# Raw weights requested as soon as their buffer is free, x loaded through ACT's queue, and fewer conversions inside the retention

## The chip, the cores and the metric

One Trainium2 chip, one of its cores. The metric is device time in microseconds (us) of one execution; smaller is better. The engines run their own instruction streams in order: TensorE (PE; its weight loads are PEld), VectorE (DVE), ScalarE (ACT), GpSimd (POOL) and SyncE (SP), which here issues the transfers.

## What is computed

Three parts follow one another on 2304 tokens (4 batches of 576) of width 512, all in float32:

```python
# 1. retention, per batch and head (8 heads of 64), gamma = 1 - 2 ** (-5 - head)
scores = q @ k.T / sqrt(64)
ret = (scores * where(i >= j, gamma ** (i - j), 0)) @ v      # -> x [2304, 512]
# 2. first feed-forward layer, w_in [512, 2048], w_out [2048, 512]
h = x @ w_in
x = (h * sigmoid(1.702 * h)) @ w_out
# 3. second feed-forward layer, w_in [512, 1024], w_out [1024, 512]
h = x @ w_in
s = h * softmax(h)
out = ((s - mean(s)) / sqrt(var(s) + 1e-6) * g_ln) @ w_out
```

The four weight matrices of parts 2 and 3 reach the core as float64, which it has to turn into float32 itself.

## The kernel before, in words

**Products.** Every operand of a matmul of parts 2 and 3 is split into a high part (a rounding copy on ACT, L291) and the rest (a subtraction on POOL or VectorE, L292), and a product is three matmuls: high x high, low x high, high x low. The up-projection is done with seven products in place of eight, on sums and differences of quarters of x and of w_in. Seven operands of x (`xop`, x0 to x6) belong to a pair of token tiles; seven combinations of w_in (`OPS`) to a slice of the weights, a window `win`.

**Steps.** Part 2 runs over 24 steps (`STEPS`): 4 generations of 4 slices of w_out, in each 3 pairs of token tiles, in each 2 halves i. A step emits h (`emit_h`: 7 products of 6 matmuls) and then y (`emit_y`: 48 matmuls; in the first two steps 24). The even step (i = 0) and the odd step (i = 1) of a pair read the same x0 to x6. During the odd step each xj becomes free after its own product; in generation 0 the next pair's xj is then computed there and stored to DRAM (`store_x`, L622), in generations 1 to 3 it is loaded back (`load_x`, L626): seven transfers of 768 KB, on SP. In h, VectorE makes the sums of products (L664) and the gated values (L638), ACT the sigmoid (L637), and ACT and POOL split the four gated tiles g11, g12, g21, g22.

**Weights.** float64 pieces of 128x512 (512 KB) are loaded by SP into one of two raw buffers (`load_raw`, L251) and turned into float32 by three integer instructions on VectorE (`convert`, L267, L270, L273), with a fourth for scaled ones. Combinations (L282), splits and, for part 3, spills of finished weights to DRAM (L392) follow.

**Order.** Each engine's order is the order in which the program emits. Background work stands in a list `bg` of (cost, function, needs, gives, late) and is emitted at calls of `slot(n)`: the head of the list goes out while its needs are done, and, if it has a cost, while n is above 0. An entry marked late is put aside and emitted first thing at the next call of `slot`. Before the change the load that refills a raw buffer is such a late entry, and so is every split and spill. `run` calls `slot` after h, after y, and in the retention's later rounds k.

**Retention.** Eight rounds k of two units (two heads each). From k = 4 on, `sums` prepares x's sums, `make_x` splits x0 to x6 for the first pair, and `slot` emits conversions.

Of the kernel before, what the change touches and what calls it, by code (L numbers as in the profile page):

```python
# [23 lines left out]
P = 128  # L24
# [80 lines left out]
RIGHT_PAD = 120  # L105
WIN = 7 * 256
# [40 lines left out]
class Build:  # L147
    def __init__(self, tc, ctx, att, consts, ident_in, w1, w2in, w2out, out):
# [13 lines left out]
        self.r2 = [rp.tile([P, LAST], F32, name="r2"), self.at(_M["c"] + _CC["qdec"][0], LAST)]  # L162
        self.dram = self.pool("dram", space=bass.MemoryType.DRAM)
# [194 lines left out]
    def next_raw(self, dst, scale=None, need=(), give=None):  # L358


        i = self.taken
        self.taken += 1
        self.queue_convert(self.raw(i), dst, scale, tuple(need) + (("raw", i),), give)
        if i + 2 < len(self.pieces):
            src = self.source(self.pieces[i + 2])
            self.add(0, lambda: self.load_raw(self.raw(i), src), (), ("raw", i + 2), True)
# [234 lines left out]
    def combine_x(self, p):  # L601
# [12 lines left out]
        def split(j, engine=None):  # L614
            x = self.xop[j]
            self.split(x[:, 0], x[:, 1], src[j], engine)
# [7 lines left out]
    def load_x(self, p, j):  # L624
        x = f32(self.xop[j].rearrange("r a k t -> r (a k t)"))
        self.nc.sync.dma_start(out=x, in_=self.xd[p][j])  # L626
# [15 lines left out]
    def emit_h(self, s):  # L642
# [44 lines left out]
        g11[2]()  # L687
        yield 3
# [16 lines left out]
        g21[0]()  # L705
        g21[1]()
# [255 lines left out]
    def run(self):  # L962
# [31 lines left out]
        def make_x(*js):  # L994
            for j in js:
                split_x(j, None)
                self.xready += 1
# [5 lines left out]
        for k in range(NPAIR):  # L1003
# [34 lines left out]
            else:  # L1038
# [7 lines left out]
                if k > 3:  # L1046
                    for _ in range((1, 1, 1, 1)[k - 4]):
                        sums.pop(0)()
                self.slot((0, 0, 0, 0, 3, 3, 3, 3)[k])
# [10 lines left out]
                if nxt:  # L1060
                    self.states(u + 3, pt)
                    self.last_masks(k + 1, ends[0])
                    self.slot(1 if k > 3 else 0)
# [9 lines left out]
            if k > 3:  # L1073
                make_x(*((), (0, 1), (2, 3), (4, 5, 6))[k - 4])

        self.open_right()
        self.slot(3)
        for g, p, i in STEPS:
# [7 lines left out]
            for j in self.emit_h(s):  # L1086
# [10 lines left out]
            self.done.add(("h", s))  # L1097
# [3 lines left out]
            if s == 0:  # L1101
                while self.first_loads:
                    load_w()
            slots = max(1, 2 * (5 - s % 6 - (g == GENS - 1)) + 2 - (g == GENS - 1))
            self.slot(7 if s == 0 else -(-self.left() // slots) + 1)
# [15 lines left out]
            self.slot(7 if s == 0 else self.left() // max(1, slots) if s + 2 < NSTEP else 0)  # L1121
# [133 lines left out]
```

## Time and profile before

| | before |
|---|---|
| median of 2 runs | 773.88 us (772.07 to 775.68) |
| profiled execution | 771.56 us, span 769.8 us |
| busy: PE, PEld, DVE, ACT, POOL | 675.1, 624.0, 533.0, 295.1, 324.1 us |
| granted clock of TensorE, mean | 0.938 of full speed |
| chain that ended last: PE, DMA, DVE | 47%, 14%, 9% of the span |
| loads of x (42 of 768 KB), median to landing | 8.7 us |
| raw w_in pieces (28 of 512 KB), median to landing | 5.0 us |

The profile is one execution; times count from its first instruction. A group of equal instructions shows their busy time, the mean of one, and the idle time of the engine before them with what ended it. The granted clock is the share of full speed (2.4 GHz) that TensorE had; 0.5 is the lower level. The chain is followed back from the last instruction, at each step to what released it. The DMA share is that of the core's 16 DMA engines.

### The profile page before, as it was taken

How to read it: one execution, taken by the hardware profiler on the slowest of the kernel's cores; microseconds unless marked ns; L12 is line 12 of the kernel's file. 1: busy time of each engine (PE TensorE's matmuls, PEld its weight loads, DVE VectorE, ACT ScalarE, POOL GpSimd, SP SyncE). 2: the span in 40 equal slices, each digit the busy share in tenths (PEclk: the TensorE clock that was granted, in tenths of full speed). 3: DMA queues.
4: the chain of work that ended last, by engine and by line, in shares of the span. 5: the costliest groups of instructions: out<-in, count | busy, mean ns of one | idle time of the engine just before them, and what ended most of it. 6: DMA issues, size and time to landing. Idle time of an engine off the chain costs nothing.

```text
span 769.8 us, 11333 instructions
## 1 busy us (share of the span) xinstructions
PE 675.1 (88%) x4326; PEld 624.0 (81%) x4326; DVE 533.0 (69%) x840; ACT 295.1 (38%) x606; POOL 324.1 (42%) x297
## 2 busy tenths in 40 slices
PE   8996567787997979997989998938989999999998
PEld 7986466787997979997989988838847888888887
DVE  3699884845556867775868656727738988778881
ACT  3564343452542333433322432314324543344431
POOL 3468662852544433453533524517513332133300
PEclk9998877898999989998999998969999999999999
DMA  9994454162136492162762283842493000000001
GB/s 346 410 376 169 175 229 164 68 259 86 39 120 249 142 357 90 55 256 112 265 242 83 61 335 110 330 148 110 157 418 125 15 17 26 28 29 29 27 28 42
DMA packets 30006, 121.78 MB, mean 158 GB/s; under 512 B 3328, under 2 KB 3840, under 8 KB 29952
## 3 DMA queue, kind: packets, MB, share of 16 engines
q1 hardware_dynamic: 29952, 121.06, 41.4%
q8 instruction: 34, 0.56, 0.3%
q14 instruction: 20, 0.16, 0.1%
HBM read 88.28 MB, written 32.77 MB: 157 GB/s over the span
## 4 chain that ended last, share of the span: by engine, by line
PE 47%; DMA 14%; DVE 9%; issue 4%; POOL 2%; ACT 2%; SPq 1%; ACTq 0%; POOLq 0%; DVEq 0%
PE o L884 13%; PE y L730 11%; PE h L794 9%; PE h_B L658 4%; PE h_C L658 4%; DMA mem<-in_w 4%; DMA mem<-in_w2out 3%; DVE mem L739 2%; PE h_D L658 2%; PE h_A L658 2%; PE zT L858 2%; DVE mem L270 2%; DVE mem L273 2%; DMA mem<-in_w2in 1%; DMA u<-wd 1%
## 5 line engine op out<-in xcount | busy, mean ns | idle before, releaser
L292 POOL TENSOR_TENSOR g<-mem,g 128x384 fp32r<-128x384 f32 x96 | 114.6, 1213 | 198.7 <-ACT g L291 188.1
L291 ACT CAST g<-mem 128x384 fp32r<-128x384 f32 x96 | 48.4, 514 | 87.9 <-DVE mem L638 87.0
L730 PE MATMUL y<-g,wo 128*128 128x384 f32 x432 | 78.2, 335 | 0.0
L730 PEld LDWEIGHTS y<-g,wo 128*128 128x128 f32 x432 | 75.6, 189 | 0.3 <-DVE mem L739 0.2
L292 POOL TENSOR_TENSOR win<-mem,win 128x256 fp32r<-128x256 f32 (+2 forms) x55 | 49.7, 933 | 56.0 <-ACT win L291 52.0
L267 DVE TENSOR_SCALAR mem<-mem 128x512 uint32<-128x512 uint32 x44 | 31.8, 723 | 55.2 <-DMA mem<-in_w 27.7
L638 DVE TENSOR_TENSOR mem<-mem 128x384 f32<-128x384 f32 x72 | 39.5, 576 | 30.1 <-ACT mem L637 30.1
L292 POOL TENSOR_TENSOR ws<-mem,ws 128x512 fp32r<-128x512 f32 (+1 forms) x36 | 44.2, 1240 | 35.2 <-ACT ws L291 35.2
L637 ACT ACTIVATE mem<-mem 128x384 f32<-128x384 f32 x72 | 36.1, 522 | 47.2 <-DVE mem L664 46.9
L658 PE MATMUL h_B<-x,win1dt.float32r 128*128 128x384 f32 x108 | 26.8, 388 | 24.3 <-DVE mem L664 16.3
L664 DVE TENSOR_TENSOR mem<-h_B,mem 128x384 f32<-128x384 f32 x48 | 26.6, 553 | 30.6 <-PE h_B L658 16.2
L794 PE MATMUL h<-ut,win 128*128 128x512 f32 x168 | 44.5, 396 | 3.0 <-DMA ut<-wdt 3.0
L270 DVE SCALAR_TENSOR_TENSOR mem<-mem 128x512 uint32<-128x512 uint32 x44 | 44.8, 1017 | 1.2
L800 DVE TENSOR_TENSOR mem<-h,mem 128x512 f32<-128x512 f32 x36 | 24.6, 688 | 30.1 <-PE h L794 17.5
L739 DVE TENSOR_TENSOR mem<-y,mem 128x384 f32<-128x384 f32 x72 | 35.7, 550 | 13.9 <-PE y L730 13.7
L658 PE MATMUL h_B<-x,win0dt.float32r 128*128 128x384 f32 x108 | 26.0, 383 | 20.8 <-DVE mem L664 20.6
L273 DVE SCALAR_TENSOR_TENSOR mem<-mem 128x512 uint32<-128x512 uint32 x44 | 43.1, 979 | 1.3
L658 PEld LDWEIGHTS h_B<-x,win1dt.float32r 128*128 128x128 f32 x108 | 21.7, 218 | 27.2 <-DVE mem L664 18.4
L884 PE MATMUL o<-u,zs 128*128 128x512 f32 (+1 forms) x171 | 41.7, 388 | 0.0
L282 DVE TENSOR_TENSOR mem<-mem 128x256 f32<-128x256 f32 (+2 forms) x49 | 40.7, 859 | 0.9
L730 PE MATMUL y<-g,wo0dt.float32r 128*128 128x384 f32 x216 | 40.7, 335 | 0.5 <-POOL g L292 0.5
L845 POOL TENSOR_TENSOR mem<-mem 128x1 f32<-128x1 f32 x18 | 10.3, 574 | 73.1 <-DVE mem L844 66.9
(144 smaller groups left out, 1629.2 us busy)
## 6 DMA issues: line engine op xcount, KB each, us to landing
x<-xd SPq DMA_DIRECT2D x42, 768.0 KB, 8.7
xd<-x SPq DMA_DIRECT2D x21, 768.0 KB, 3.9
mem<-in_w SPq DMA_DIRECT2D x28, 512.0 KB, 5.0
in<-in_att SPq DMA_DIRECT2D x16, 576.0 KB, 8.5
in<-in_att SPq DMA_DIRECT2D x16, 544.0 KB, 8.9
out<-mem SPq DMA_DIRECT2D x17, 256.0 KB, 2.0
mem<-in_w2out SPq DMA_DIRECT2D x8, 512.0 KB, 3.8
wd<-ws SPq DMA_DIRECT2D x8, 512.0 KB, 5.1
```

The lines of the kernel that those rows point to most:

```text
L270: lambda: nc.vector.scalar_tensor_tensor(high, high, 0xC0000000, x, ALU.bitwise_and, ALU.bitwise_or),
L273: lambda: nc.vector.scalar_tensor_tensor(x, low, 29, high, ALU.logical_shift_right, ALU.bitwise_or),
L282: self.nc.vector.tensor_tensor(o, a, b, ALU.subtract)
L291: self.nc.scalar.copy(hi, src)
L292: (engine or self.nc.gpsimd).tensor_tensor(lo, src, f32(hi), ALU.subtract)
L637: lambda: nc.scalar.activation(g, src, AF.Sigmoid, scale=1.702),
L638: lambda: nc.vector.tensor_tensor(g, src, g, ALU.mult),
L658: nc.tensor.matmul(o, w[:, c:c + P], x[j][:, m, k], start=(start and i == 0), stop=(stop and i == 5), skip_group_check=True,)
L730: nc.tensor.matmul(self.yps[m], w[:, c:c + P], gs[:, b], start=(begin and i == 0), stop=(end and i == 2),)
L739: nc.vector.tensor_tensor(y[:, m], self.yps[m], y[:, m], ALU.add)
L794: nc.tensor.matmul(o, a[:, l, k], w[:, m], start=(start and i == 0), stop=(stop and i == 5), skip_group_check=True,)
L884: nc.tensor.matmul(o[:, 0:n], z[:, a, k], w[:, b, p * n:(p + 1) * n], start=(k == 0 and i == 0), stop=(k == FB - 1 and i == 2),)
```

## The change

It does five things. (1) `next_raw`: the load that refills a raw buffer is emitted as soon as the conversion that read it has been emitted; only the mark that allows its conversion is put off to the next `slot`. (2) `load_x`: the 42 loads of x are issued by ACT in place of SP. (3) `emit_h` itself calls `slot`: once without budget after g11's split, which emits what was put off, and once with the budget of the step between g21's sigmoid and its product; the call after h is gone. (4) In the retention the background budgets go from 3, 3, 3, 3 (rounds 4 to 7) and 1, 1, 1 to 3, 3, 3, 0 and none, then 5 in place of 3 before part 2, and 8.4 and 6 in place of 7 and 7 in step 0; x0 to x6 are made in another order and earlier, and the last of the first raw loads go out ahead of step 0's stores. (5) x's subtraction is issued as two of 128x384 in place of one of 128x768, and 56 words of padding stand at the end of the retention's tiles.

```diff
+RET_PAD = 56
...
+        rp.tile([P, RET_PAD], F32, name="rpad")
...
         if i + 2 < len(self.pieces):
             src = self.source(self.pieces[i + 2])
-            self.add(0, lambda: self.load_raw(self.raw(i), src), (), ("raw", i + 2), True)
+            self.add(0, lambda: self.load_raw(self.raw(i), src))
+            self.add(0, lambda: None, (), ("raw", i + 2), True)
...
         def split(j, engine=None):
             x = self.xop[j]
-            self.split(x[:, 0], x[:, 1], src[j], engine)
+            a = src[j] if len(src[j].shape) == 3 else src[j].rearrange("r (k t) -> r k t", k=2)
+            self.nc.scalar.copy(x[:, 0], a)
+            for k in range(2):
+                (engine or self.nc.gpsimd).tensor_tensor(x[:, 1, k], a[:, k], f32(x[:, 0, k]), ALU.subtract)
...
         x = f32(self.xop[j].rearrange("r a k t -> r (a k t)"))
-        self.nc.sync.dma_start(out=x, in_=self.xd[p][j])
+        self.nc.scalar.dma_start(out=x, in_=self.xd[p][j])
...
-    def emit_h(self, s):
+    def emit_h(self, s, n_slot):
...
         g11[2]()
+        self.slot(0)
         yield 3
...
         g21[0]()
+        self.done.add(("h", s))
+        self.slot(n_slot)
         g21[1]()
...
                 if k > 3:
-                    for _ in range((1, 1, 1, 1)[k - 4]):
-                        sums.pop(0)()
-                self.slot((0, 0, 0, 0, 3, 3, 3, 3)[k])
+                    sums.pop(0)()
+                self.slot((0, 0, 0, 0, 3, 3, 3, 0)[k])
...
-                    self.slot(1 if k > 3 else 0)
+                    self.slot(0)
...
             if k > 3:
-                make_x(*((), (0, 1), (2, 3), (4, 5, 6))[k - 4])
+                make_x(*((1, 3), (0, 2), (4, 6), (5,))[k - 4])
 
         self.open_right()
-        self.slot(3)
+        self.slot(5)
...
-            for j in self.emit_h(s):
+            slots = max(1, 2 * (5 - s % 6 - (g == GENS - 1)) + 2 - (g == GENS - 1))
+            for j in self.emit_h(s, 8.4 if s == 0 else -(-self.left() // slots) + 1):
+                while s == 0 and self.first_loads:
+                    load_w()
...
-            self.done.add(("h", s))
             if g == 0 and i == 0 and after is not None:
                 for fn in sums[:3]:
                     fn()
-            if s == 0:
-                while self.first_loads:
-                    load_w()
-            slots = max(1, 2 * (5 - s % 6 - (g == GENS - 1)) + 2 - (g == GENS - 1))
-            self.slot(7 if s == 0 else -(-self.left() // slots) + 1)
...
-            self.slot(7 if s == 0 else self.left() // max(1, slots) if s + 2 < NSTEP else 0)
+            self.slot(6 if s == 0 else self.left() // max(1, slots) if s + 2 < NSTEP else 0)
```

TensorE's order is the same in both. Where the change moves instructions is shown at three places; lines are those of each kernel's own text.

First SP, from the end of generation 0's stores (`xd`) to the first spill (`wd`) in generation 1; `in_w` and `in_w2out` are raw weights, x<-xd the loads of x. Before:

```order
L622 DMA xd_6_152<-x_131 128x1536
L251 DMA mem<-in_w 128x1024 x5
L626 DMA x_125<-xd_0_139 128x1536
L626 DMA x_126<-xd_1_140 128x1536
L626 DMA x_127<-xd_2_141 128x1536
L626 DMA x_128<-xd_3_142 128x1536
L626 DMA x_129<-xd_4_143 128x1536
L626 DMA x_130<-xd_5_144 128x1536
L626 DMA x_131<-xd_6_145 128x1536
L251 DMA mem<-in_w 128x1024 x2
L251 DMA mem<-in_w2out 128x1024 x3
L392 DMA wd_0_111<-ws 128x1024
```

With the change:

```order
L628 DMA xd_5_152<-x_131 128x1536
L253 DMA mem<-in_w 128x1024
L628 DMA xd_6_153<-x_132 128x1536
L253 DMA mem<-in_w 128x1024 x6
L253 DMA mem<-in_w2out 128x1024 x3
L395 DMA wd_0_112<-ws 128x1024
L253 DMA mem<-in_w2out 128x1024
```

The loads of x are gone from SP, so that raw loads and spills follow one another directly; in generation 0 a raw load now stands ahead of the last store.

Second ACT, in step 9 (odd, generation 1): C11 (L672, L678) and C22 (L677, L683) are the first products taken out of PSUM, ACTIVATE the sigmoids, ws the split for a spill. Before, from the cast for the spill at the end of step 8:

```order
L291 CAST ws<-mem 128x512
L672 COPY mem<-h_A 128x384
L677 COPY mem<-h_C 128x384
L637 ACTIVATE mem<-h_A 128x384
L291 CAST g_1087<-mem 128x384
L637 ACTIVATE mem<-mem 128x384 x2
L291 CAST g_1088<-mem 128x384
L291 CAST g_1090<-mem 128x384
L637 ACTIVATE mem<-mem 128x384
L291 CAST g_1089<-mem 128x384
```

With the change:

```order
L293 CAST ws<-mem 128x512
L632 DMA x_126<-xd_0_133 128x1536
L678 COPY mem<-h_A 128x384
L632 DMA x_127<-xd_1_134 128x1536
L683 COPY mem<-h_C 128x384
L632 DMA x_128<-xd_2_135 128x1536
L643 ACTIVATE mem<-h_A 128x384
L293 CAST g_1086<-mem 128x384
L632 DMA x_129<-xd_3_136 128x1536
L632 DMA x_130<-xd_4_137 128x1536
L643 ACTIVATE mem<-mem 128x384 x2
L293 CAST g_1087<-mem 128x384
```

Each load of x stands behind the instruction that follows its product, and the first of them behind the cast for the spill.

Third VectorE, from the end of step 0's h (L664, L670 with h_D) to the conversion after the next window's combinations (128x256). L638 and L644 are g21's product; the rows of 128x768 and 128x2x384 are the sums for the next pair's x. Before:

```order
L664 TENSOR_TENSOR mem<-h_D,mem 128x384
L638 TENSOR_TENSOR mem<-mem 128x384
L610 TENSOR_TENSOR mem<-mem 128x768
L282 TENSOR_TENSOR mem<-mem 128x768
L282 TENSOR_TENSOR mem<-mem 128x2x384
L270 SCALAR_TENSOR_TENSOR wo3dt.uint_122<-wo3dt.uint_122,mem 128x512
L273 SCALAR_TENSOR_TENSOR mem<-wo3dt.uint_122 128x512
L282 TENSOR_TENSOR mem<-mem 128x256 x4
L267 TENSOR_SCALAR mem<-mem 128x512
```

With the change:

```order
L670 TENSOR_TENSOR mem<-h_D,mem 128x384
L269 TENSOR_SCALAR mem<-wo2dt.uint_122 128x512
L272 SCALAR_TENSOR_TENSOR wo2dt.uint_122<-wo2dt.uint_122,mem 128x512
L275 SCALAR_TENSOR_TENSOR mem<-wo2dt.uint_122 128x512
L269 TENSOR_SCALAR mem<-wo3dt.uint_123 128x512
L272 SCALAR_TENSOR_TENSOR wo3dt.uint_123<-wo3dt.uint_123,mem 128x512
L275 SCALAR_TENSOR_TENSOR mem<-wo3dt.uint_123 128x512
L284 TENSOR_TENSOR mem<-mem 128x256 x4
L269 TENSOR_SCALAR mem<-mem 128x512
L644 TENSOR_TENSOR mem<-mem 128x384
```

Two pieces (wo2, wo3) are converted here in place of before h, g21's product stands behind the conversions, and the sums of x behind g21. Up to step 1's first sum 24 conversion instructions are issued in place of 27, up to step 4's 40 in place of 42; from step 5 on the counts agree.

## Rows read from the trace of the kernel before

**Rows 1.** Busy us by stage: PE, PEld, DVE, ACT, POOL; PEclk, DMA share, GB/s
```profile
72.00:177.30 105.30, 72.78 (x341) 68.42 (x337) 75.21 (x91) 45.12 (x84) 59.91 (x38) 0.81 0.47 177
177.30:240.00 62.70, 62.70 (x350) 62.57 (x351) 34.89 (x55) 28.18 (x58) 28.83 (x23) 0.97 0.33 123
240.00:478.80 238.80, 213.47 (x1152) 210.60 (x1151) 168.68 (x269) 80.65 (x157) 101.41 (x81) 0.94 0.46 170
478.80:555.90 77.10, 59.92 (x325) 57.93 (x324) 48.26 (x76) 25.43 (x52) 38.60 (x34) 0.91 0.50 187
555.90:584.00 28.10, 21.66 (x79) 13.56 (x78) 12.45 (x19) 7.29 (x16) 4.09 (x6) 1.00 0.97 392
584.00:769.80 185.80, 182.78 (x900) 153.63 (x900) 140.62 (x250) 75.24 (x158) 51.03 (x66) 1.00 0.07 26
```

**Rows 2.** Chain that ended last, in order of time: start us, us, what
```profile
182.59 8.32 PE y L730 x48
190.91 1.04 PE h_B L658 x6
...
229.93 11.60 DMA mem<-in_w
...
269.89 14.13 DMA mem<-in_w2out
...
448.33 11.09 DMA mem<-in_w2in
```

**Rows 3.** Timeline of PE: start us, us, what [idle before <-releaser]
```profile
247.14 2.29 PE L658 MATMUL h_B<-x,win 128*128 128x384 f32 x6 [5.18 <-DVE mem L664]
...
465.50 2.29 PE L658 MATMUL h_B<-x,win0dt.float32r 128*128 128x384 f32 x6 [5.13 <-DVE mem L664]
```

**Rows 4.** Timeline of SP, its issues, around two sets of x loads
```profile
223.27 6.56 SPq L626 DMA_DIRECT2D x<-xd  x7
229.93 5.65 SPq L251 DMA_DIRECT2D mem<-in_w  x2
...
264.21 5.58 SPq L626 DMA_DIRECT2D x<-xd  x7
269.89 0.38 SPq L251 DMA_DIRECT2D mem<-in_w2out  x1
```

**Rows 5.** Timeline of DVE: two waits for weights, two ends of conversions
```profile
126.13 0.43 DVE L267 TENSOR_SCALAR mem<-mem 128x512 uint32<-128x512 uint32 x1 [9.25 <-DMA mem<-in_w]
...
174.88 0.43 DVE L267 TENSOR_SCALAR mem<-mem 128x512 uint32<-128x512 uint32 x1 [8.51 <-DMA mem<-in_w]
...
219.38 0.69 DVE L273 SCALAR_TENSOR_TENSOR mem<-mem 128x512 uint32<-128x512 uint32 x1
...
264.81 0.69 DVE L273 SCALAR_TENSOR_TENSOR mem<-mem 128x512 uint32<-128x512 uint32 x1
```

**Rows 6.** Groups by shape: xcount | busy us, mean ns | idle
```profile
L273 DVE SCALAR_TENSOR_TENSOR mem<-mem 128x512 uint32<-128x512 uint32 x44 | 43.1, 979 | 1.3
...
L292 POOL TENSOR_TENSOR g<-mem,g 128x384 fp32r<-128x384 f32 x96 | 114.6, 1213 | 198.7 <-ACT g L291 188.1 <-PE h_B L658 8.0 <-PE y L730 1.4
...
L292 POOL TENSOR_TENSOR x<-mem,x 128x768 fp32r<-128x768 f32 x15 | 30.2, 2031 | 4.3 <-ACT x L291 4.3
```

**Rows 7.** Source line 626, the loads of x: duration ns min/median/max, landing
```profile
L626 SPq DMA_DIRECT2D x<-xd x42: 319/320/732, 223.3 to 489.5; - x42
...
DMA to landing us min/median/max: 4.1/8.7/13.1
```

**Rows 8.** Timelines of ACT, DVE and PE in steps 21 and 22
```profile
503.97 0.62 ACT L291 CAST ws<-mem 128x512 fp32r<-128x512 f32 x1 [10.11 <-DMA wdb<-ws]
...
511.61 0.43 DVE L267 TENSOR_SCALAR mem<-mem 128x512 uint32<-128x512 uint32 x1 [10.94 <-DMA mem<-in_w2in]
...
515.08 2.29 PE L658 MATMUL h_B<-x,win0dt.float32r 128*128 128x384 f32 x6 [8.37 <-DVE mem L664]
```


## The prediction

> **What bounds the kernel now.** I read the stages first, then the chain of waits, then what stood behind each stall of TensorE on SP and on VectorE. A step below is one up-projection h (42 matmuls) and one down-projection y (48 matmuls); there are 24, numbered from 0, six to a generation.
>
> The stages [rows 1] say where TensorE is not the bound. From 584 to 769.8 us it is busy 182.78 of 185.80 us at full clock: that stage is its own bound, and the change does not touch it. From 72 to 177.3 us it is busy 72.78 of 105.30 us at a granted clock of 0.81, from 240 to 478.8 us 213.47 of 238.80 us at 0.94, from 478.8 to 555.9 us 59.92 of 77.10 us at 0.91. The loss sits in these three.
>
> The chain [rows 2] shows what a step costs when nothing is late: 48 matmuls of y in 8.32 us and six of h in 1.04 us, so 8.32 + 7 x 1.04 = 15.6 us. It also holds five long transfers of raw weights, 11.09 to 14.13 us each (the first, the longest and the last are shown). After each, TensorE stood still before the fifth product of an h; of these five stalls the first and the last are shown, 5.18 and 5.13 us, waiting for VectorE's sum, and the six matmuls behind them take 2.29 us in place of 1.04, the lower clock level (1.2 GHz) after a pause [rows 3]. VectorE is late because it works in order and a conversion ahead of the sum waits for its weights. SP's queue shows why these are late [rows 4]: x's seven loads go out first (223.27, 264.21 us) and hold SP for 6.56 and 5.58 us, since each waits for the matmuls that read its buffer; the raw load behind them leaves at 229.93 and 269.89 us. Yet its buffer was free at 220.1 and 265.5 us, when the last conversion that read it ended [rows 5]. Seven x loads are 5.5 MB, 14.0 us at the 392 GB/s of [rows 1]; that is what the raw load then shares the engines with.
>
> **Part A, steps 0 to 4: -19 us.** VectorE is the tight engine here: 75.21 us of 105.30 [rows 1], and it waited 9.25 us (to 126.13) and 8.51 us (to 174.88) for raw weights [rows 5] that stood on SP behind x's stores. In the new order the loads stand ahead of the stores and each conversion a slot or more later, so I take both waits out: 17.8 us. Up to step 4's first sum 40 conversion instructions are issued in place of 42, so 2 x 0.69 us [rows 5] go too. Sum 19.2, taken as 19. Four conversions fewer stand ahead of the first h, so that one starts sooner, but VectorE still has to do them before step 1, and I count nothing for them. The sums of the next pair's x, now behind the first window's conversions, are the same case. Ends: 9 us if one of the two waits only changes its place, 23 if the four conversions are won as well (4 x 0.98 us [rows 6]).
>
> x's subtraction in two halves: 2 x 1.21 us for 2.03 on POOL, 15 times, 6 us [rows 6]. POOL is busy 59.91 of 105.30 us, and x is made a pair of units earlier in the retention; cost nothing, 6 us if it stands in the way. The 56 words of padding move tiles and add no instruction; no row shows what a place costs. I bound it by the spread of one conversion, 0.3 us (0.98 less 0.69), either way for some 20 instructions, 6 us, and take nothing.
>
> **Part B, steps 8 to 20: -36 us.** Thirteen steps of 15.6 us are 202.8 us; they took from 237.8 us (247.14 less its stall and four products) to 478.8, 241.0 us. So 38.2 are lost, and the five stalls with their slow matmuls are nearly all of it. With x on ACT's queue and the raw load issued as soon as its buffer is free, it leaves at about 220 and 265.5 us. It landed at 241.5 and 284.0 us (issue plus length [rows 2]) with VectorE some 5 us in wait, so it is due at about 236 and 279, at least 13 us after the new issue; even with all of x ahead the slowest took 14.13. I take 36 and leave 2 for sums queued behind conversions that are not late. Ends: 18 (half of it stays in shorter stalls) and 38.
>
> What is late next: x itself. A buffer of x is free after its own product in the odd step and read 15.6 us later in the next; from the first free buffer to the last use are 15.6 + 6 x 1.04 = 21.8 us, for 14.0 us of loads and some 2.7 us for two raw loads. So x fits with 5 us to spare. The last of the seven stands on ACT behind the last g of the step, and that behind the conversions now put between the sigmoid and its product: about 4 x 0.98 + 3 x 0.55 = 5.6 us later than on SP. That takes up the 5 us, and I expect waits under 1 us. ACT issues 42 loads at 0.32 us, 2.2 us in a step that has them [rows 7]; ACT is busy 80.65 of 238.80 us [rows 1], which covers it; if the evacuations came that much later, 6 x 2.2 = 13 us.
>
> **Part C, steps 21 to 23 and the last y: -8 us.** They take 77.1 us where 3 x 15.6 + 8.32 = 55.1 would do: 22.0 lost. Two long waits stand there: ACT 10.11 us for a spill's write behind x's loads, VectorE 10.94 us for raw weights, and TensorE 8.37 us behind the latter [rows 8]. The spill no longer queues behind x, but the last two raw loads still follow seven spills on SP, and three spills of step 21 now stand on ACT ahead of x's fourth load and of the sigmoids. Ends 0 and 17 (8.37 us twice); I take the middle, 8.
>
> **Sum.** The profiled execution took 771.56 us (span 769.80): 771.6 - 19 - 36 - 8 = 708.6 us. The median of the runs shown, 773.88, is 2.3 above it: **711 us**.
>
> A rule speaks against the move of x: the Trainium skill, DMA: Bandwidth & Descriptors, section Rules for kernel authors, says that spreading transfers over SP, ACT and GpSimd adds no bandwidth, since all run on the same 16 engines. If that were the whole of it, only the earlier request would count, and the time would be that of rival 2. The same page of the Trainium skill, section Queues, rings and completion order, has each engine alternate between the queues it has work for, so that a raw load would not stand behind all of x. No run here shows two queues at work: all of this kernel's transfers go through SP's.
>
> **Rivals.**
> 1. VectorE becomes the bound (0.14). Its 168.68 us of work from 240 to 478.8 us [rows 1] are 83% of 202.8, and 75.21 are 87% of 86.3 (105.3 - 19). Its in-order waits for ACT's sigmoid come on top, and a conversion has a mean of 0.98 us against 0.69 undisturbed [rows 5, 6]. Against: TensorE ran 62.70 us without a gap from 177.3 to 240 [rows 1]. Half of each part is kept: 771.6 - 32 + 2.3 = 742 us.
> 2. The queue does not matter, and a raw load still waits for the x loads issued before it (0.10). Of the two buffers shown one was free before x's first load and one after [rows 4, 5], so I let two of five stalls go, 2/5 of 36 = 14: 771.6 - 19 - 14 + 2.3 = 741 us.
> 3. ACT is held by its loads (0.08). If an issue lasted as long as its transfer (786 KB at 392 GB/s, 2.0 us), seven would take 14 us, 7 more than an h; g would be 7 us late for the y behind it, with 1 of slow clock 8, in each of six sets: 771.6 - 63 + 48 + 2.3 = 759 us. Against: the longest x issue on SP took 0.73 us [rows 7].
> 4. Slower: x's loads lose their cover (0.06). Place: the h after each of the six sets. ACT takes its stream in order; if a cast ahead of x's first load waits as long as ACT's 10.11 us [rows 8] and the g chain holds the last loads, x starts when TensorE has little left to do. Price: all 14.0 us of a set and 2.5 of slow clock (two groups at 2.29 for 1.04), 16.5 x 6 = 99: 771.6 - 63 + 99 + 2.3 = 810 us. It decides from 10.5 us uncovered in a set (63 / 6). Against: only three of the six sets have a spill's cast directly ahead.
>
> That the raw loads are not asked for sooner, the change not doing what it says, I exclude: the new order puts them ahead of x's stores and apart from x's loads.
>
> **How the numbers follow.** My forecast has 0.62. Its own range, the ends taken as independent: up by the root of 10² + 18² + 8², 22, down by that of 4² + 2² + 9² + 6², 12, so 699 to 733. Rivals 1 and 2 are faster too, rival 3 is within 2% (15.5 us, about what a measurement of this kernel can tell from no change), rival 4 slower: faster 0.86, within 0.08, slower 0.06. The range runs from 690 (all good ends at once, 771.6 - 78 + 2.3 = 696, and 6 for the padding) to 750 (rivals 1 and 2, with as much again as the padding's 6 and 2 of spread between runs); it leaves out rivals 3 and 4 and some tails, about 0.2.
>
> **What would show it.** In the new profile: no long transfer of raw weights in the chain between 160 and 480 us; VectorE's conversions (L267 before) idle for weights below 10 us in all, where [rows 5] alone have 17.8; the granted clock of the middle stage near 1.00; step 4's fifth product at about 158 us in place of 177.3, the first transposes at about 521 in place of 584. Rival 1 would show TensorE waiting for VectorE and VectorE at 95%; rival 2 raw loads that take over 10 us to land; rivals 3 and 4 TensorE waiting for g or for x's loads in the even steps. The forecast fails if x's loads land later than the 21.8 us allow, or if the retention, whose order also changes, gets longer by more than part A wins.

## The result and the profile after

The changed kernel took **732.69 us** (median of two runs, 730.73 and 734.65) beside 773.88 before: ratio 0.947, 95% interval 0.932 to 0.961. The forecast was 711, its range 690 to 750. The profiled execution took 730.73 us (span 728.9). Against the forecast's own sum for a profiled execution, 708.6, 22.1 us are missing.

The stages of the changed kernel, cut at the same places of the program as [rows 1] and with the same columns:

```profile
69.00:162.20 93.20, 69.46 (x341) 64.98 (x338) 79.11 (x98) 42.97 (x82) 63.47 (x49) 0.89 0.46 173
162.20:222.70 60.50, 60.50 (x351) 60.50 (x350) 40.75 (x64) 28.57 (x59) 28.05 (x23) 1.00 0.40 145
222.70:435.70 213.00, 203.24 (x1152) 200.54 (x1151) 169.21 (x263) 78.80 (x157) 98.53 (x81) 0.99 0.51 190
435.70:514.30 78.60, 63.42 (x326) 61.23 (x324) 44.03 (x76) 24.77 (x52) 36.95 (x35) 0.89 0.49 182
514.30:543.20 28.90, 21.61 (x78) 13.56 (x78) 12.36 (x19) 8.04 (x16) 4.60 (x7) 1.00 0.96 389
543.20:728.90 185.70, 182.78 (x900) 153.62 (x900) 140.55 (x250) 75.22 (x158) 50.99 (x66) 1.00 0.07 26
```

The first stage went from 105.3 to 93.2 us, the middle one from 238.8 to 213.0 with its clock from 0.94 to 0.99. The stage with the last steps did not gain: 77.1 before, 78.6 now. The two stages behind it took 0.7 us longer together.

For all kernels below I use three numbers, read from TensorE's timeline by the first product of each step: when step 5 starts (part A), how long steps 8 to 20 take (part B; 15.6 us a step would be 202.8) and steps 21 to 23 with the last y (part C; 55.1 at best). Before: 190.8, 242.3, 76.1. Now: **173.5, 216.5, 77.5**, so -17.3, -25.8 and +1.4, where the forecast had -19, -36 and -8.

The chain of waits (start us, us, what) shows what is left of the long transfers of [rows 2]:

```profile
206.19 5.37 DMA mem<-in_w
...
254.54 10.61 DMA x<-xd
...
415.52 7.29 DMA mem<-in_w2in
...
441.07 8.65 DMA wdt<-ws
...
461.68 8.77 DMA mem<-in_w2in
```

Five raw transfers of 11 to 14 us up to step 20 have become two, 5.37 us and, ahead of step 20's stall, 7.29. New are a load of x (10.61) and, in step 22, the last two pieces of w2in (8.77); a spill's write (8.65) stood in the chain of before too, with 8.05 us. The groups by shape that answer to [rows 6] (xcount | busy us, mean ns | idle), and the loads of x that answer to [rows 7] (ns min/median/max, first and last start):

```profile
L272 DVE SCALAR_TENSOR_TENSOR mem<-mem 128x512 uint32<-128x512 uint32 x44 | 42.5, 965 | 1.2
L275 DVE SCALAR_TENSOR_TENSOR mem<-mem 128x512 uint32<-128x512 uint32 x44 | 42.2, 958 | 1.2
L269 DVE TENSOR_SCALAR mem<-mem 128x512 uint32<-128x512 uint32 x44 | 33.7, 767 | 12.3 <-DMA mem<-in_w2in 7.2 <-POOL ws L294 3.1 <-DMA mem<-in_w 2.0
```

```profile
L632 ACTq DMA_DIRECT2D x<-xd x42: 326/327/801, 205.9 to 462.2; - x42
```

VectorE now waits 7.2 + 2.0 = 9.2 us for weights in the whole kernel, where before it was 51.9 (in [rows 5] two waits alone made 17.8). A conversion costs about what it did (its third instruction 958 ns on average for 979). ACT issues a load of x in 0.33 us, as SP did, at most 0.80: rival 3 is out.

TensorE's stalls of the changed kernel that answer to [rows 3], with the columns of that group:

```profile
227.51 1.36 PE L664 MATMUL h_B<-x,win 128*128 128x384 f32 x6 [2.90 <-DVE mem L670]
```

```profile
265.20 1.15 PE L664 MATMUL h_D<-x,win 128*128 128x384 f32 x5 [1.72 <-DMA x<-xd]
```

```profile
328.48 1.31 PE L664 MATMUL h_B<-x,win1dt.float32r 128*128 128x384 f32 x6 [2.67 <-DVE mem L670]
```

```profile
472.21 2.29 PE L664 MATMUL h_B<-x,win0dt.float32r 128*128 128x384 f32 x6 [6.74 <-DVE mem L670]
```

In steps 8 and 14 TensorE still waits for VectorE's sum, about half as long as before, with no weight late; in step 10 it waits for x; in step 22 the old long wait stands with its slow matmuls (2.29 us for six, the 1.2 GHz level).

### The profile page after: what moved, and what is told of

Its sections match the earlier page's. It is cut to its first block, busy times and chain, and to the rows that moved or that the text cites. A ratio compares the mean times of both kernels' runs of the same rounds, so it can differ in the third digit from the quotient of the medians.

```text
span 728.9 us, 11371 instructions
## 1 busy us (share of the span) xinstructions
PE 664.2 (91%) x4326; PEld 613.3 (84%) x4326; DVE 536.6 (74%) x846; ACT 292.4 (40%) x606; POOL 324.1 (44%) x312
## 3 DMA queue, kind: packets, MB, share of 16 engines
q1 hardware_dynamic: 23904, 88.03, 31.7%
## 4 chain that ended last, share of the span: by engine, by line
PE 58%; DVE 22%; DMA 11%; ACT 5%; issue 3%; POOL 2%; SPq 0%; ACTq 0%; POOLq 0%; DVEq 0%
PE y L739 15%; PE o L893 14%; PE h L803 9%; PE h_B L664 4%; PE h_C L664 3%; DVE mem L272 3%; PE h_A L664 3%; DVE mem L284 3%; DVE mem L275 3%; DVE mem L644 2%; DVE mem L269 2%; DMA mem<-in_w2in 2%; PE zT L867 2%; DVE mem L670 2%; PE h_D L664 2%
## 5 line engine op out<-in xcount | busy, mean ns | idle before, releaser
L294 POOL TENSOR_TENSOR g<-mem,g 128x384 fp32r<-128x384 f32 x96 | 109.0, 1147 | 195.7 <-ACT g L293 172.4
L644 DVE TENSOR_TENSOR mem<-mem 128x384 f32<-128x384 f32 x72 | 46.7, 676 | 27.1 <-ACT mem L643 27.1
L294 POOL TENSOR_TENSOR ws<-mem,ws 128x512 fp32r<-128x512 f32 (+1 forms) x36 | 41.5, 1166 | 25.1 <-ACT ws L293 25.1
L748 DVE TENSOR_TENSOR mem<-y,mem 128x384 f32<-128x384 f32 x72 | 36.5, 551 | 18.6 <-PE y L739 18.2
L809 DVE TENSOR_TENSOR mem<-h,mem 128x512 f32<-128x512 f32 x36 | 24.6, 687 | 31.6 <-PE h L803 17.5
L739 PE MATMUL y<-g,wo1dt.float32r 128*128 128x384 f32 x216 | 42.0, 343 | 2.4 <-ACT g L293 2.4
L670 DVE TENSOR_TENSOR mem<-h_B,mem 128x384 f32<-128x384 f32 x48 | 26.5, 551 | 23.8 <-ACT mem L678 14.8
L272 DVE SCALAR_TENSOR_TENSOR mem<-mem 128x512 uint32<-128x512 uint32 x44 | 42.5, 965 | 1.2
L275 DVE SCALAR_TENSOR_TENSOR mem<-mem 128x512 uint32<-128x512 uint32 x44 | 42.2, 958 | 1.2
L269 DVE TENSOR_SCALAR mem<-mem 128x512 uint32<-128x512 uint32 x44 | 33.7, 767 | 12.3 <-DMA mem<-in_w2in 7.2
L803 PEld LDWEIGHTS h<-ut,win 128*128 128x128 f32 x168 | 30.8, 188 | 13.3 <-DMA ut<-wdt 6.7
L739 PEld LDWEIGHTS y<-g,wo1dt.float32r 128*128 128x128 f32 x216 | 39.1, 195 | 2.7 <-ACT g L293 2.7
```

The costliest lines, as they stand in the source:

```text
L269: lambda: nc.vector.tensor_scalar(x, high, 3, 0x3FFFFFF8, ALU.logical_shift_left, ALU.bitwise_and),
L272: lambda: nc.vector.scalar_tensor_tensor(high, high, 0xC0000000, x, ALU.bitwise_and, ALU.bitwise_or),
L275: lambda: nc.vector.scalar_tensor_tensor(x, low, 29, high, ALU.logical_shift_right, ALU.bitwise_or),
L294: (engine or self.nc.gpsimd).tensor_tensor(lo, src, f32(hi), ALU.subtract)
L644: lambda: nc.vector.tensor_tensor(g, src, g, ALU.mult),
L670: add = lambda o, a, b: nc.vector.tensor_tensor(o, a, b, ALU.add)
```

## The experiments

Each kernel was timed beside the kernel before on the same chip, so ratios to it compare. Diffs are cut to the lines that count. Each experiment has four runs, the changed kernel two.

| kernel | time us | ratio to before, 95% | step 5 at | steps 8 to 20 | steps 21 to 23 |
|---|---|---|---|---|---|
| before | 773.88 | 1 | 190.8 | 242.3 | 76.1 |
| changed | 732.69 | 0.947 (0.932 to 0.961) | 173.5 | 216.5 | 77.5 |
| 1 early request alone | 761.47 | 0.988 (0.983 to 0.992) | 185.5 | 236.5 | 77.2 |
| 2 ACT's queue alone | 747.09 | 0.968 (0.964 to 0.973) | 190.2 | 218.3 | 76.4 |
| 3 both | 741.46 | 0.961 (0.956 to 0.965) | 182.7 | 216.6 | 76.9 |
| 4 changed, slot back | 749.02 | 0.970 (0.964 to 0.975) | 189.6 | 219.3 | 78.2 |
| 5 changed, old retention | 735.40 | 0.952 (0.947 to 0.956) | 176.7 | 216.0 | 79.2 |
| 6 five spill buffers | 729.20 | 0.945 (0.942 to 0.948) | 176.4 | 216.2 | 73.6 |
| 7 less work on POOL | 727.10 | 0.943 (0.939 to 0.946) | 174.8 | 210.2 | 79.2 |
| 8 x's last load earlier | 734.95 | 0.953 (0.949 to 0.956) | 174.6 | 217.4 | 79.1 |
| 9 last raw pieces early | 732.50 | 0.951 (0.948 to 0.953) | 176.8 | 218.2 | 72.3 |
| 10 9, and 6 for all spills | 718.30 | 0.932 (0.928 to 0.935) | 175.5 | 215.8 | 64.0 |
| 11 10 and y's splits later | 714.17 | 0.925 (0.920 to 0.930) | 173.3 | 217.4 | 60.4 |
| 12 no padding | 735.83 | 0.954 (0.952 to 0.957) | 176.0 | 218.6 | 78.1 |

The columns by part come from one profile each. The changed kernel and numbers 6 to 11 run the same program up to step 5, and it starts between 173.3 and 176.8 us: a difference under 3.5 us in part A says nothing from one profile. Up to step 18 numbers 6, 9, 10 and 11 still run the changed kernel's program, and their middle takes 215.8 to 218.2 us beside its 216.5: one under 2.4 us says nothing there either.

### Which half of the change wins the middle: 1, 2 and 3

```diff
-            self.add(0, lambda: self.load_raw(self.raw(i), src), (), ("raw", i + 2), True)
+            self.add(0, lambda: self.load_raw(self.raw(i), src))
+            self.add(0, lambda: None, (), ("raw", i + 2), True)
```

> Before plus the earlier request for raw weights alone; x's loads stay on SP's queue, the order of conversions and the retention stay as before. Theory Q (x's loads on SP's queue are what held the raw loads in steps 8 to 20): a raw load now stands ahead of x's loads on SP, but x's loads then wait behind it for the conversion that frees its buffer, so steps 8 to 20 win little, 5 of the 25.8 us; steps 0 to 4, where x's stores stood ahead, win most of their 17: about 774 - 5 - 14 = 755 us. Rival R (asking sooner is the whole of it, the queue does not matter): steps 8 to 20 win all 25.8 as well, about 733 us.

761.47 us; steps 8 to 20 win 5.8 us. Theory Q holds there, rival R falls; steps 0 to 4 win 5.3, not 14, which is more than the 6 us that Q is out by. SP's timeline of this kernel, then its chain, show why the middle stays slow:

```profile
254.09 5.56 SPq L627 DMA_DIRECT2D x<-xd  x7
259.74 0.39 SPq L251 DMA_DIRECT2D mem<-in_w2out  x1
```

```profile
259.74 14.55 DMA mem<-in_w2out
276.79 2.29 PE h_B L659 x6
```

Asked for early or not, this raw load still stands on SP behind seven loads of x and lands 14.55 us later.

```diff
-        self.nc.sync.dma_start(out=x, in_=self.xd[p][j])
+        self.nc.scalar.dma_start(out=x, in_=self.xd[p][j])
```

> Before plus x's loads on ACT's queue alone; raw weights asked for a slot later as before. Theory Q: steps 8 to 20 win nearly all of the 25.8 us, because on SP nothing but spills stands ahead of a raw load any longer, and a slot later in the program is no later in time when nothing ahead waits; steps 0 to 4 have no loads of x and win nothing: about 774 - 24 = 750 us. Rival R: the raw load is still asked for late and shares the engines with x, steps 8 to 20 win under 10 us: 765 us or more.

747.09 us, steps 8 to 20 in 218.3: 24.0 of the 25.8 us that the whole change wins there. SP's timeline of this kernel, to be held against [rows 4]:

```profile
219.55 15.55 SPq L251 DMA_DIRECT2D mem<-in_w  x2
240.97 15.27 SPq L251 DMA_DIRECT2D mem<-in_w2out  x3
```

The first load of [rows 4] left at 229.93 us, after x's; here it leaves at 219.55, without having been asked for any earlier in the program. The time to landing of its raw loads:

```profile
DMA to landing us min/median/max: 3.5/5.3/10.5
```

Before it was 3.6, 4.9 and 14.1: the longest is shorter, the median is not. The rule of the Trainium skill (DMA: Bandwidth & Descriptors, Rules for kernel authors) that more queues add no bandwidth is not contradicted: the bytes are the same. What the second queue removed is a place in line, and here that was worth 24.0 us. Whether the engines also take turns between the two queues shows little: of the 13 raw loads that were issued here with x in flight, one landed ahead of a load of x issued before it (3 of 18 in the changed kernel, none of 10 in the kernel before).

> Before plus the earlier request and x's loads on ACT's queue; conversions at their old places and the retention as before. If these two are the whole change in effect (theory Q with the stores' part): 774 - 17 - 26 = 731 to 735 us, within 3 us of the changed kernel. If the slot that moved into h or the smaller share of conversion in the retention carries part of it: 742 us or more. If the moved slot costs (sums wait behind conversions, x's last load stands behind them): 728 us or less.

741.46 us, just under the 742 of the second reading, that the moved slot or the lighter retention carries part of it. The middle is that of the changed kernel to 0.1 us (216.6): these two make all of it, x's queue 24.0; the early request's 1.7 on top is within the 2.4 that profiles differ by. Step 5 starts at 182.7, 9.2 later than in the changed kernel, which speaks for the second reading.

### Which part wins the beginning: 4 and 5

```diff
-        self.slot(0)
         yield 3
...
-        self.slot(n_slot)
         g21[1]()
...
+            self.slot(n_slot)
```

> The changed kernel with the slot of conversions put back behind the whole h (behind the last g's product and cast) and without the late work after the first g. Theory: x's seventh load no longer stands behind the conversions on ACT's side, so step 10's wait of 1.72 us for x goes, and the last g is no longer late; the conversions come some 2 us later: -4 to +2 us, 729 to 735 us. Rival S (conversions a slot sooner are what removes the waits for VectorE): steps 8, 14 and 20 lose 3 us each more and step 4 its wait comes back: +10 to +18, 743 to 751 us.

The last line goes behind the loop over the products of h. 749.02 us: my theory fell. Of rival S the wait in step 4 came back (25.2 us for 18.4), the 3 us in each of steps 8, 14 and 20 did not: steps 8 to 20 lose 2.8 together, and 16.1 lie ahead of step 5: step 0 takes 25.5 us for 20.9, step 1 33.1 for 25.6, step 4 25.2 for 18.4. SP's timeline, then VectorE's, then TensorE's:

```profile
152.19 17.64 SPq L628 DMA_DIRECT2D xd<-x  x7
169.93 1.35 SPq L253 DMA_DIRECT2D mem<-in_w  x2
```

```profile
175.32 0.43 DVE L269 TENSOR_SCALAR mem<-mem 128x512 uint32<-128x512 uint32 x1 [5.28 <-DMA mem<-in_w]
```

```profile
117.03 0.69 PE L736 MATMUL y<-g,wo2dt.float32r 128*128 128x384 f32 x1 [11.23 <-ACT wo2dt.float32r L293]
```

With the slot behind h the raw loads stand behind all seven stores of x again, and a wait like those of [rows 5] is back. In step 1 TensorE waits 11.23 us for an output weight, wo2.

```diff
-                    sums.pop(0)()
-                self.slot((0, 0, 0, 0, 3, 3, 3, 0)[k])
+                    for _ in range((1, 1, 1, 1)[k - 4]):
+                        sums.pop(0)()
+                self.slot((0, 0, 0, 0, 3, 3, 3, 3)[k])
...
-                    self.slot(0)
+                    self.slot(1 if k > 3 else 0)
...
-                make_x(*((1, 3), (0, 2), (4, 6), (5,))[k - 4])
+                make_x(*((), (0, 1), (2, 3), (4, 5, 6))[k - 4])
```

> The changed kernel with the retention of before: its old shares of conversion, the old order in which x is made, step 0's slots of 7; the slot inside h, the early request and ACT's queue for x stay. It fills the fourth corner: step 5 starts at 182.7 us with neither the moved slot nor the lighter retention, at 189.6 with the retention alone, at 173.5 with both. Theory I (the two only pay together: the conversions taken from the retention need the slot inside h): step 5 starts at 180 to 183 us, the run takes 737 to 742 us. Theory J (the slot inside h pays by itself, the lighter retention costs 7 us as it does without it): step 5 starts at 173 or before, 725 to 732 us.

735.40 us, step 5 at 176.7, between the two theories and inside the spread of the changed kernel's program. So with the old retention the slots inside h win 6.0 us (182.7 to 176.7), with the lighter one 16.1 (189.6 to 173.5). The lighter retention wins nothing that one profile can show beside them; without them it lost 6.9 (182.7 to 189.6). In the 6.0 and the 6.9 are also x's subtraction in halves, the padding and the place of the first loads, which experiments 1 to 3 do not have.

By step, the 17.3 us lie at the start (step 0 begins at 69.1 us for 72.3; 67.8 to 71.8 in the seven profiles), in step 1 (25.6 for 32.7) and in step 4 (18.4 for 24.7). Step 1 takes 24.8 to 26.0 us in all kernels with the slots inside h, 32.6 to 33.6 before and in experiments 1 to 4. ACT and TensorE in the kernel before, in steps 1 and 4:

```profile
118.06 0.61 ACT L291 CAST wo3dt.float32r<-mem 128x512 fp32r<-128x512 f32 x1
118.73 0.69 PE L730 MATMUL y<-g,wo3dt.float32r 128*128 128x384 f32 x1 [5.95 <-ACT wo3dt.float32r L291]
121.53 3.89 PE L730 MATMUL y<-g,wo3dt.float32r 128*128 128x384 f32 x11 [2.12 <-POOL wo3dt.float32r L292]
...
177.28 2.29 PE L658 MATMUL h_B<-x,win0dt.float32r 128*128 128x384 f32 x6 [6.90 <-DVE mem L664]
```

And in the changed kernel, step 1:

```profile
104.32 0.61 ACT L293 CAST wo3dt.float32r<-mem 128x512 fp32r<-128x512 f32 x1
111.78 4.02 PE L739 MATMUL y<-g,wo3dt.float32r 128*128 128x384 f32 x12 [3.24 <-ACT g L293]
```

The conversion of wo3 had ended at 90.1 us before and ends at 86.3 now. Its split is a late entry: before, it went out behind the whole h of step 1; now it goes out at the slot behind g11's split. In experiment 4, without that slot, it starts at 116.9 us again, 25 us behind its conversion. No run has one of the two slots alone. The wait of 6.90 us in step 4 is gone in the changed kernel, and 1.83 with the early request alone (20.1 us for 24.7).

```diff
-        rp.tile([P, RET_PAD], F32, name="rpad")
```

> The changed kernel without the 56 words of padding behind the retention's tiles: tiles behind them move, no instruction changes. Forecast's step (the place costs nothing, bounds 6 us either way): 728 to 734 us, steps and waits as in the changed kernel. Rival (the place sets the price of VectorE's conversions): steps 0 to 8 differ by 4 us or more, 735 to 738 us.

735.83 us, outside what I wrote by 2, with step 5 at 176.0 and steps 8 to 20 in 218.6. Neither reading is met: the time is the rival's, but the steps 0 to 8 don't show its 4 us, and the three instructions of a conversion cost 765, 987 and 975 ns on average for 767, 965 and 958, so the place does not set their price. Whether the padding's place wins some 3 us stays open.

### What is left in the middle: 7 and 8

```diff
-                self.split(w[:, a:b], w[:, WIN + a:WIN + b], self.at(_M["stg"] + a, b - a))
+                if n < 3:
+                    self.split(w[:, a:b], w[:, WIN + a:WIN + b], self.at(_M["stg"] + a, b - a))
+                else:
+                    self.nc.scalar.copy(w[:, a:b], self.at(_M["stg"] + a, b - a))
```

> The changed kernel without POOL's low part of the windows from the fourth on (15 subtractions left out; the matmuls read what an earlier window left there, so their number and shape stay). Theory P (in steps 8, 14 and 20 the conversions ahead of VectorE's sum are slowed by POOL's subtraction of the window beside them, 2.27 and 1.50 us where 0.69 and 0.43 are normal): the waits of 2.90, 2.67 and 1.61 us for VectorE there fall below 1 us, with the slow matmuls behind them some 3 us each: 722 to 727 us. Rival N (the conversions are too many there, whatever POOL does): the waits keep at least two thirds of their size, 729 to 733 us.

727.10 us, just above theory P's range; steps 8 to 20 in 210.2, 6.3 less. Step 8 takes 15.6 us for 20.3 and its wait is gone, step 14 16.5 for 18.5 with a wait of 0.62 for 2.67; step 20 keeps 17.4 of 17.5, so there theory P is wrong (its conversions wait for a weight of w2in, the 7.29 us of the chain). Step 8 in the changed kernel, VectorE and then POOL:

```profile
221.62 2.27 DVE L275 SCALAR_TENSOR_TENSOR mem<-mem 128x512 uint32<-128x512 uint32 x1
223.82 1.50 DVE L269 TENSOR_SCALAR mem<-mem 128x512 uint32<-128x512 uint32 x1
225.36 1.63 DVE L272 SCALAR_TENSOR_TENSOR mem<-mem 128x512 uint32<-128x512 uint32 x1
226.91 0.54 DVE L670 TENSOR_TENSOR mem<-h_B,mem 128x384 f32<-128x384 f32 x1
```

```profile
221.51 4.93 POOL L294 TENSOR_TENSOR win1dt.float32r<-mem,win1dt.float32r 128x768 fp32r<-128x768 f32 x3
```

And VectorE in the same place of experiment 7:

```profile
222.79 0.68 DVE L275 SCALAR_TENSOR_TENSOR mem<-mem 128x512 uint32<-128x512 uint32 x1
224.04 0.43 DVE L269 TENSOR_SCALAR mem<-mem 128x512 uint32<-128x512 uint32 x1 [0.57 <-DMA mem<-in_w]
224.51 0.69 DVE L272 SCALAR_TENSOR_TENSOR mem<-mem 128x512 uint32<-128x512 uint32 x1
225.12 0.55 DVE L673 TENSOR_TENSOR mem<-h_B,mem 128x384 f32<-128x384 f32 x1
```

The three instructions take 1.80 us alone and 5.40 beside POOL's subtractions (the row holds three of them, one of 128x768 and two of 128x512). The 3.60 more cover the wait of 2.90 us. The subtractions end at 223.35, 225.04 and 226.44 us, the conversion's instructions at 223.90, 225.32 and 226.99: each 0.3 to 0.6 us behind a subtraction, as if it had waited for its end. The Trainium skill (SBUF — State Buffer, section SBUF: two separate sides) says that VectorE with two inputs in SBUF and a GpSimd operation that reads it lock each other out; the two instructions with two inputs agree. The one with a single input (1.50 for 0.43) was slowed too.

```diff
+        if g:
+            yield 6
         self.slot(n_slot)
         g21[1]()
         g21[2]()
-        yield 6
+        if not g:
+            yield 6
```

> The changed kernel with x's seventh load issued ahead of the slot of conversions and of the last g's product and cast, from the second generation on. Theory X (the last load of x is late in step 10 because it stands on ACT behind the cast that waits for the conversions): the wait of 1.72 us for x in step 10 goes, with the slow matmuls behind it 2.7 us, and 0.7 us in step 16: 727 to 730 us. Rival: x lands late because the engines are full of x's six other loads, the spill and the raw loads: no change, 731 us.

734.95 us (0.949 to 0.956 of before), above both readings, though the changed kernel's interval takes it in. The wait for x in step 10 fell from 1.72 to 0.52 and step 10 from 18.3 to 17.2, so the load's place on ACT was part of it; but step 14 took 20.0 for 18.5 (its wait of 2.69 was followed by slow matmuls this time, as it is in experiments 6, 9 and 11, which change nothing there), and the middle as a whole did not move (217.4). No gain is shown.

### Where part C's 8 us went: 6, 9, 10 and 11

The places that answer to [rows 8] in the changed kernel, ACT and then VectorE:

```profile
449.80 0.62 ACT L293 CAST ws<-mem 128x512 fp32r<-128x512 f32 x1 [4.82 <-DMA wdt<-ws]
```

```profile
456.32 1.02 DVE L644 TENSOR_TENSOR mem<-mem 128x384 f32<-128x384 f32 x2 [7.95 <-ACT mem L643]
...
468.41 0.43 DVE L269 TENSOR_SCALAR mem<-mem 128x512 uint32<-128x512 uint32 x1 [4.43 <-DMA mem<-in_w2in]
```

In step 21 ACT's casts wait for the write of the spill before them, the sigmoids behind them are late, VectorE waits for those, and its conversions release the raw buffers late.

```diff
         w = self.ws[:, i % 2]
+        k = (i - 8) % 5
+        if 8 <= i < 15 and k < 3:
+            w = self.win[2][:, k * SLICE:(k + 1) * SLICE].rearrange("r (a b) -> r a b", a=2)
```

> The changed kernel with five spill buffers for the first seven spills of the second layer's input weights: three lie in the third window, which is idle after step 17. Theory W (part C is lost because ACT's casts wait mid-h for the write of the one spill that still holds the buffer, which makes the sigmoids late, then VectorE's conversions, then the last two raw loads): ACT's waits of 4.82, 1.83 and 1.58 us in step 21 go, steps 21 to 23 fall from 77.5 to 65 to 70 us, the run to 721 to 727 us. Rival D (the transfers themselves are the bound there, 374 to 433 GB/s from 436 to 455 us: x's seven loads, seven spills and two raw loads share the engines): the wait only moves, steps 21 to 23 stay within 3 us, 728 to 733 us.

729.20 us, in rival D's range, and half right. Step 21 falls from 24.3 to 17.5 us, but step 22 rises to 26.2 and step 23 to 29.9; 73.6 for 77.5. Rival D's 374 to 433 GB/s belong to an earlier place, 410 to 423 us; from 436 to 455 us the changed kernel moved 262 GB/s on average. The chain of this kernel shows where the wait went:

```profile
453.71 12.02 DMA mem<-in_w2in
469.30 2.29 PE h_B L667 x6
```

The load left when its buffer was free, not when SP was: SP's last spill issue ended at 452.2 us, the conversion that read the buffer at 453.7. Experiment 9 gives the last two pieces another place (raw2, where the third window was):

```diff
+        k = i - len(self.pieces) + 2
+        if k >= 0:
+            return self.raw2[:, k * SLICE:(k + 1) * SLICE]
...
+        for k in ([i + 2] if i < n - 6 else [i + 2, i + 4] if i < n - 4 else []):
```

> The changed kernel with the last two raw pieces of the second layer's input weights loaded into the third window's place, idle after step 17, and asked for ahead of the seven spills on SP, while their old buffers are still full. With five spill buffers the wait had moved to these two loads (12.02 us, beside x's loads and the spills). Theory V (part C is two waits in a row: ACT's casts for the spill buffers in step 21, then the last two raw loads in step 22): step 22 falls from 25.2 to 16 to 18 us, step 21 stays near 24, the run takes 722 to 725 us. Rival (the engines are full whatever the order, or the next spill is late instead): steps 21 to 23 stay within 3 us of 77.5, 729 to 733 us.

732.50 us, steps 21 to 23 in 72.3: step 22 falls from 25.2 to 19.6, step 21 stays at 25.2. The part's number speaks for theory V; the total is the rival's, 8 above what I wrote, 3.3 of it from a step 5 at the late end of the spread.

Experiment 10 takes both edits, with the idle places of three output weights as the further spill buffers, now for all fourteen spills.

> The changed kernel with both: the last two raw pieces in the third window's place and asked for early, and five spill buffers for all fourteen spills of that matrix (three of them the output weights' places that are idle after step 18). Theory V: both waits go, step 21 takes 17 to 18 us, step 22 16 to 18, step 23 with the last y 25 to 28: 60 to 64 in place of 77.5, the run 715 to 719 us. Rival: one of the two waits comes back behind x's loads, 70 us or more, 724 us or more.

**718.30 us**, as theory V has it, steps 21 to 23 in 64.0, the steps 17.5, 17.2 and 29.3 (the last 1 above its range). In these steps the two edits alone won 3.9 and 5.2, together 13.5; in the total alone 3.5 and 0.2, inside the spread, together 14.4. They are two waits in a row, and taking one away lets the other grow. The seven further spills add nothing to that: they are cast from 470 us on, behind step 22's h, and step 23 is no shorter (29.3 for 28.0). TensorE's last waits there:

```profile
444.07 1.33 PE L682 MATMUL h_B<-x,win1dt.float32r 128*128 128x384 f32 x6 [1.60 <-DVE mem L688]
461.32 1.34 PE L682 MATMUL h_B<-x,win0dt.float32r 128*128 128x384 f32 x6 [1.35 <-DVE mem L688]
479.37 2.29 PE L682 MATMUL h_A<-x,win1dt.float32r 128*128 128x384 f32 x6 [3.18 <-ACT mem L696]
```

Experiment 11 takes the last of these three waits too: y's splits (all but the four sums of ys) go behind the last slot of step 23's h.

```diff
-                for fn in ys:
+                for fn in ys[:4]:
...
+                for fn in ys[4:]:
+                    fn()
```

> The kernel with both edits of the last stage (early raw pieces, five spill buffers), and the seven splits of y's operands for the second layer moved from ahead of step 23 to behind its h. Theory: in step 23 TensorE waits 3.18 us for ACT's copy of the second product, because seven casts (2.24 us, themselves behind VectorE's sums) stand ahead of it on ACT; with the casts behind h the wait and the six slow matmuls (2.29 for 1.04) go, 4.4 us, and nothing needs them for the 16 us of two y: 713 to 715 us. Rival (the loads of the second layer's weights end last in any case): the wait only moves to the first products there, 717 to 719 us.

**714.17 us**, ratio 0.925 (0.920 to 0.930): better than the kernel before and the changed one, intervals apart (from experiment 10's they are not). In step 23 the wait for ACT is gone, this is the first one left:

```profile
477.70 1.31 PE L682 MATMUL h_B<-x,win1dt.float32r 128*128 128x384 f32 x6 [0.33 <-DVE mem L688]
```

## Why the prediction was right, and where it was short

**Part A, -19 forecast, -17.3 measured** (-14.0 at the late end of the spread). The size was right, its working only in part, and that part was luck. I set the two waits of 9.25 and 8.51 us equal to the gain. Experiment 1 removes both (VectorE's longest wait for weights there is 1.16 us) and wins 5.3: an idle VectorE was not TensorE's loss one for one. The second wait cost TensorE 6.90 us in step 4; the first cost it nothing that shows, since steps 1 and 2 take 33.6 and 16.4 us without it, 32.7 and 16.8 with it. In its place came 7.1 us in step 1, from splits that go out inside h, and 3.2 from a first h that starts sooner: the first stood nowhere in my sum, the second I counted as nothing. That the lighter retention and the padding are worth nothing fits experiments 5 and 12 within 3 us.

**Part B, -36 forecast, -25.8 measured.** The mechanism was right: the queue is what held the raw loads (24.0 us in experiment 2), and they leave when their buffer is free. The step that failed is "I take 36 and leave 2 for sums queued behind conversions that are not late": 13.7 us remain above 202.8. Of these 6.3 went with POOL's split of the next window, which slows the conversion just ahead of a sum threefold. [Rows 5, 6] held 0.69 us undisturbed and 0.98 on average for an instruction of it; ahead of the sum the three took 1.50 to 2.27. "Waits under 1 us" for x was short too: 1.72 in step 10.

**Part C, -8 forecast, +1.4 measured.** Experiments 1 to 5 all lie between 76.4 and 79.2: no part of the change wins anything there. The slots inside h only move some 6 us from step 22 to step 21 (25.2 and 24.3 us; 29.7 to 31.7 and 17.8 to 18.1 before and in experiments 1 to 4). The step that failed is "I take the middle, 8": it had no mechanism behind it. Of the two obstacles I named, spills on ACT ahead of the sigmoids are one that decides (experiment 6); the last raw loads were late for their full buffers more than for the seven spills ahead of them on SP. Experiments 6, 9 and 10 show that either alone pays less than half of both.

The three terms miss 1.7, 10.2 and 9.4 us, the tail 0.7: 22.0 of the 22.1.

**The rivals.** Rival 1 (VectorE the bound) did not come as a whole, VectorE is busy 169.21 of 213.00 us, 79%; but its mark, TensorE waiting for VectorE's sum, is what is left in steps 8 and 14. Rival 2 falls with experiment 2: the queue alone wins 24.0 us of the middle, the early request alone 5.8. Rival 3 left no trace; of rival 4 there is one, the 1.72 us for x in step 10. **The marks:** long raw transfers in the chain between 160 and 480 us (not gone: 5.37, 7.29 and 8.77 us are left), waits for weights 9.2 us (right, below 10), the middle's clock 0.99 (right), step 4's fifth product at 162.1 us for 158, the first transposes at 543.2 for 521 (both late).

## What to carry to other kernels

A queue is an order: before a load is asked for sooner, see what stands ahead of it on the queue and what that waits for. Here moving the waiting transfers to another queue was worth 24.0 us of the middle, asking sooner on top of it no more than profiles differ by. A wait taken from an engine off the critical path is not a gain of its own length, and where two waits stand in a row only both together pay in full (3.9 and 5.2 apart, 13.5 together). A weight that is converted but not yet split is still late: emitting put-off splits inside h won 7.1 us in one step. Cost an operation by what its neighbours do at that moment, not by its mean.

## What the runs showed of the hardware

A conversion on VectorE with one input in SBUF, 0.43 us alone, took 1.50 beside POOL's subtractions of 128x768 and 128x512; those with two inputs went from 0.68 and 0.69 to 2.27 and 1.63. After the same wait of 2.66 to 2.69 us in step 14, TensorE's granted clock stayed at 1.00 in the changed kernel and experiment 10 (the step took 18.5 and 18.6 us) and fell to the lower level in experiments 6, 9 and 11 (20.0 to 20.1), with the same program up to there. The same program ahead of step 5 ended up to 3.5 us apart in seven profiles.
